# A sparse attention with two MLPs: the first block's weight conversion held to three units ahead of use, and the opening loads reordered

## The chip, the core and the metric

One NeuronCore of a Trainium2 chip. Five engines run their own instruction streams and meet at semaphores: PE (TensorE, matrix multiply), DVE (VectorE, elementwise), ACT (ScalarE, elementwise with functions), POOL (GpSimd) and SP (SyncE, which issues most DMAs). PEld is PE's weight load, which overlaps its matmuls. The metric is device time of one execution in microseconds (us), lower is better.

## The reference

```
scores = q @ k.T / sqrt(64)           # 4 batches, 8 heads, 576 positions, head size 64
heads 0-3: keep 0 <= i - j < 32       # local
heads 4-7: keep j <= i, i % 32 == j % 32   # strided
x  = softmax(scores) @ v              # as 2304 tokens x 512
x  = (s * relu(x @ w_in)**2 + b) @ w_out          # w_in 512x2048, w_out 2048x512, float64
out = ((x @ w_a) * (x @ w_b)) @ w_o2              # w_a, w_b 512x1536, w_o2 1536x512, float64
```

The weights arrive as float64 and are converted on the core, and every float32 product is made of three passes of a split high + low operand (`PASSES`).

## The kernel before

The 2304 tokens are cut into six blocks of 384. Block 0 holds positions 0 to 95 of the four batches, block 1 positions 96 to 191, and blocks 2 to 5 the rest of one batch each.

**First attention.** `first` computes block 0's attention, one batch at a time: `first_load` (L331) brings q and k (tile `fqk`) and v (`fv`) of a batch, 192 KB each; PE transposes them (`fps`), multiplies scores (`fss`), DVE and ACT make the softmax (`fpt`, L210 to L223), PE transposes that (`fpp`) and multiplies with v (`fpo`); the result is split into the high and low half of `x`.

**The first MLP** goes through the hidden dimension in 16 units of 128 columns (NF1 = 16). For block n and unit f, `h_mm` makes 12 matmuls into `h`, ACT takes relu and square, and the result is split into `gt` (ACT writes the high half, DVE the low one, L132); `o_mm` of unit f - 2 (AHEAD1 = 2) adds 12 matmuls into `acc`. PE's order is written out: h(f), then steps of the next block's attention, then acc(f - 2), then more attention steps, and each step follows the last PE instruction (`in_order`). The attention of block n + 1 is made of two generators, `local_gens` and `strided_gens`; for block 1 each has four pieces, spread over the 16 units. Their tiles are `qn`, `kn`, `vn`, `lpt` (local) and `sk`, `sv`, `spo`, `spTo` (strided), `pqk`, `pst`, `pss`, `ppt` and `po` in PSUM.

**The weights** of a unit are two raw tiles of 512 KB, one of w_in and one of w_out (`stage`, L139 and L144), each with two 32-bit words per value. `to_float32` turns a raw tile into a float32 tile: ACT scales the high word (L153), DVE shifts and merges (L157, L160, L163), and `split` writes the high half on ACT (L131) and the low half on DVE (L132) of a tile `w`. `next_weights` does this for the two tiles of the next unit and stages raw tiles up to two units further.

In the kernel before, `stage_next` runs twice first, with the four raw loads of units 0 and 1 on ACT's DMA queue; the q, k and v loads follow on SP's. After the first attention two units are converted, and in block 0 `next_weights` stands inside the order of unit f, with only one condition: it comes after the last batch of the first attention. The scheduler then orders each engine's instructions by readiness, except for what is tied by `tc.issue_after` or raised by `tc.high_priority`.

From block 1 on, streams convert the second MLP's weights and write them to DRAM (`convert_w2`), and sum columns (`column_sums`). The last part of the program is the second MLP (`ab_mm`, `o2_mm`), which is matmuls nearly alone.

Of the kernel before, what the change touches and what calls it, by code (L numbers as in the profile page):

```python
# [26 lines left out]
def sparse_attention_two_mlps(  # L27
# [22 lines left out]
    nc = tc.nc  # L50
    B, H, S, D = q.shape
# [16 lines left out]
    NF1 = FF1 // P  # L68
# [41 lines left out]
    last_pe, behind = [], []  # L110
# [20 lines left out]
        nc.scalar.activation(out=hi, in_=src, func=AF.Copy)  # L131
        return eng_lo.tensor_tensor(out=lo, in0=src, in1=hi.bitcast(F32), op=ALU.subtract)  # L132

    def stage(w, f, cols, pool, queue=nc.sync):

        r = pool.tile([P, DM, 2], U32, tag="w" if pool in (wpa, wpb) else "raw", name="raw")
        words = w.bitcast(U32)
        if cols:
            load = queue.dma_start(  # L139
                out=r.rearrange("p (k c) t -> p k (c t)", k=KD),  # L140
                in_=words[:, f * 2 * P:(f + 1) * 2 * P].rearrange("(k p) c -> p k c", p=P),
            )
        else:
            load = queue.dma_start(  # L144
                out=r.rearrange("p c t -> p (c t)"), in_=words[f * P:(f + 1) * P, :]
            )
        return r, load.ins
# [182 lines left out]
    def first_load(dst, src, bb):  # L330
        nc.sync.dma_start(out=dst, in_=src[bb, :, 0:QT, :].rearrange("h t d -> t h d"))  # L331
# [214 lines left out]
    wi, wo = {}, {}  # L546
# [164 lines left out]
        gens = [strided(n - 2, pair) for pair in range(2)]  # L711
        return overlapped(gens, 4), 2 + 13 * len(gens)

    AHEAD1, AHEAD2 = 2, 1
    NX = 3 * NF2 - 2 * NF1
    words = []
    last_load = None

    def stage_next():

        nonlocal last_load
        f = len(words)
        both = []

        for w, cols, pool in (
            (w_in, True, raw if f >= NF1 - 1 else wpa), (w_out, False, raw if f >= NF1 - 2 else wpb)
        ):
            with tc.issue_after(last_load) if last_load is not None else ExitStack():

                r, load = stage(w, f, cols, pool, nc.scalar if f < 2 else nc.sync)  # L730
            last_load = load if f >= 2 else None
            both.append(r)
        words.append(both)

    def next_weights():
        f = len(wi)
        while len(words) <= min(NF1 - 1, f + 2):
            stage_next()
        wi[f] = by_rows(to_float32(words[f][0], wpa, "w"))
        wo[f] = to_float32(words[f][1], wpb, "w")  # L740
# [22 lines left out]
    qks, vs = [], []  # L763
    for bb in range(B):
# [1 line left out]
            vf = slot(wpb, [QT, 2, H, D], "fv")  # L766
        vs.append(vf[:, bb % 2])
        qks.append(slot(wpb, [QT, 2, H, D], "fqk"))
    for _ in range(2):
        stage_next()  # L770
    for bb in range(B + 2):
        if bb < B:
            first_load(qks[bb][:, 0], q, bb)
            first_load(qks[bb][:, 1], k, bb)
        if bb >= 2:
            first_load(vs[bb - 2], v, bb - 2)
    banks = ((ps_acc, "acc"), (ps_a, "a"), (ps_acc, "acc"), (ps_a, "a"))
    gens = [first(bb, qks[bb], vs[bb], fmask, *banks[bb]) for bb in range(B)]
    live, step = list(range(B)), 0
    while live:  # L780

        live = [bb for bb in live if bb > step or next(gens[bb], gens) is not gens]
        step += 1
    for _ in range(2):
        next_weights()
    later = [
        Stream(convert_w2(), 3 * NF2 + 1, (NB - 2) * NF1 - 2), Stream(column_sums(), NF1 + 1, 2 * NF1 - 1)
# [2 lines left out]
    for n in range(NB):  # L790
# [12 lines left out]
        for f in range(NF1):  # L803
            order = ExitStack()
            if n == 0:

                order.enter_context(tc.issue_after(first_done[B - 1].ins))
                if len(wi) < NF1:
                    next_weights()
            gt = in_order(h_mm, n, f)  # L810
            for st in streams:
                st()
            queue.append((acc, gt, f, n))
            if len(queue) > AHEAD1:
                in_order(o_mm, *queue.pop(0))
            for st in streams:
                st()
            order.close()
            if n == NB - 1:
                while len(w2) < NX + 2 * (f + 1 - AHEAD1):  # L820
                    load_w2(len(w2))
            elif n:
                for st in later[:n]:
                    st()
# [50 lines left out]
```

## Time and profile before

| | |
|---|---|
| median of 3 runs | 1057.99 us (1057.22 to 1059.37) |
| the profiled execution | 1055.04 us |
| its span in the profile | 1053.3 us |
| PE busy | 993.7 us (94%) |
| DVE busy | 473.4 us (45%) |
| ACT busy | 462.5 us (44%) |
| POOL busy | 74.8 us (7%) |
| first matmul of block 0's first unit | 45.20 us |
| first matmul of block 1's first unit | 169.50 us |

Times in the trace are us from the start of the span. A line of a timeline gives start, duration, engine, line of the code, operation, tile written <- tiles read, shapes and count, and in brackets how long the engine had been idle before it and what ended that. The span is 1.7 us shorter than the execution it was taken from.

### The profile page before, as it was taken

How to read it: one execution, taken by the hardware profiler on the slowest of the kernel's cores; microseconds unless marked ns; L12 is line 12 of the kernel's file. 1: busy time of each engine (PE TensorE's matmuls, PEld its weight loads, DVE VectorE, ACT ScalarE, POOL GpSimd, SP SyncE). 2: the span in 40 equal slices, each digit the busy share in tenths (PEclk: the TensorE clock that was granted, in tenths of full speed). 3: DMA queues.
4: the chain of work that ended last, by engine and by line, in shares of the span. 5: the costliest groups of instructions: out<-in, count | busy, mean ns of one | idle time of the engine just before them, and what ended most of it. 6: DMA issues, size and time to landing. Idle time of an engine off the chain costs nothing.

```text
span 1053.3 us, 15817 instructions
## 1 busy us (share of the span) xinstructions
PE 993.7 (94%) x5984; PEld 932.9 (89%) x5984; DVE 473.4 (45%) x1246; ACT 462.5 (44%) x1291; POOL 74.8 (7%) x110
## 2 busy tenths in 40 slices
PE   4958699999999899999999999999999999999998
PEld 3747599999999889999999999999999999999997
DVE  5799642767778777766622221221211211211111
ACT  4787565665765667476532231311311311211212
POOL 4000000000223331200000000000000000000000
PEclk9988699999999999999999999999999999999999
DMA  9675212254654635554567720100200100000000
GB/s 189 201 240 185 76 39 71 81 170 129 196 152 146 183 125 147 153 174 148 174 207 234 254 85 1 50 11 1 60 1 1 61 1 1 30 1 1 30 1 30
DMA packets 109819, 106.37 MB, mean 101 GB/s; under 512 B 59568, under 2 KB 94640, under 8 KB 109744
## 3 DMA queue, kind: packets, MB, share of 16 engines
q1 hardware_dynamic: 103216, 84.39, 28.0%
q0 software_dynamic: 5184, 18.88, 4.6%
q10 hardware_dynamic: 1344, 2.10, 0.6%
q8 instruction: 47, 0.77, 0.3%
q14 instruction: 28, 0.23, 0.1%
HBM read 77.03 MB, written 28.31 MB: 100 GB/s over the span
## 4 chain that ended last, share of the span: by engine, by line
PE 80%; DVE 8%; ACT 5%; DMA 4%; issue 2%; POOL 0%; SPq 0%; ACTq 0%; DVEq 0%; POOLq 0%
PE acc L113 29%; PE h L113 16%; PE pb L113 14%; PE pa L113 14%; PE pss L113 2%; PE po L113 2%; DVE raw L163 2%; DVE w L132 2%; DVE raw L160 1%; PE ppt L116 1%; DMA xr<-o 1%; DVE raw L157 1%; DMA fqk<-in_q_dram 1%; PE fss L113 1%; ACT w L131 1%
## 5 line engine op out<-in xcount | busy, mean ns | idle before, releaser
L113 PE MATMUL h<-x,w 128*128 128x384 f32 x1152 | 225.7, 344 | 1.8 <-ACT r L560 1.2
L113 PE MATMUL acc<-gt,w 128*128 128x384 f32 x1152 | 223.5, 341 | 2.7 <-ACT o1s L586 2.7
L113 PEld LDWEIGHTS h<-x,w 128*128 128x128 f32 x1152 | 202.5, 191 | 5.9 <-ACT r L560 2.0
L113 PEld LDWEIGHTS acc<-gt,w 128*128 128x128 f32 x1152 | 199.9, 189 | 6.9 <-ACT o1s L586 3.4
L641 DVE TENSOR_TENSOR ab<-pb,ab 128x384 f32<-128x384 f32 x72 | 40.1, 557 | 306.6 <-ACT ab L640 306.6
L113 PE MATMUL pb<-x,w 128*128 128x384 f32 x864 | 164.8, 337 | 0.0
L113 PE MATMUL pa<-x,w 128*128 128x384 f32 x864 | 161.9, 334 | 0.8 <-ACT ab L640 0.8
L113 PE MATMUL acc<-w,abt 128*128 128x512 f32 x648 | 161.8, 393 | 0.0
L640 ACT ACTIVATE ab<-pa 128x384 f32<-128x384 f32 x72 | 35.4, 491 | 282.3 <-PE pa L113 282.2
L113 PEld LDWEIGHTS pb<-x,w 128*128 128x128 f32 x864 | 153.7, 188 | 6.1
L113 PEld LDWEIGHTS pa<-x,w 128*128 128x128 f32 x864 | 150.8, 188 | 1.6 <-ACT ab L640 1.4
L113 PEld LDWEIGHTS acc<-w,abt 128*128 128x128 f32 x648 | 120.5, 188 | 21.9
L560 ACT ACTIVATE r<-h 128x384 f32<-128x384 f32 x96 | 46.6, 486 | 115.5 <-PE h L113 115.2
L567 DVE TENSOR_TENSOR r<-r 128x384 f32<-128x384 f32 x80 | 48.6, 608 | 88.6 <-ACT gt L566 88.0
L132 DVE TENSOR_TENSOR abt<-ab,abt 128x384 fp32r<-128x384 f32 x72 | 40.2, 558 | 46.9 <-ACT abt L131 46.9
L131 ACT ACTIVATE w<-raw 128x512 fp32r<-128x512 f32 x68 | 44.9, 668 | 27.3 <-DVE raw L163 20.6
L132 DVE TENSOR_TENSOR w<-raw,w 128x512 fp32r<-128x512 f32 x68 | 46.4, 686 | 22.1 <-ACT w L131 21.6
L568 DVE TENSOR_TENSOR gt<-r,gt 128x384 fp32r<-128x384 f32 x80 | 54.1, 676 | 4.5
L131 ACT ACTIVATE abt<-ab 128x384 fp32r<-128x384 f32 x72 | 37.7, 524 | 40.2 <-DVE ab L641 40.2
L604 POOL DMA_DIRECT2D w2d<-w x36 | 20.0, 556 | 443.6 <-DVE w L132 370.0
L153 ACT ACTIVATE raw<-raw 128x512 f32<-128x512 f32 x68 | 45.1, 674 | 9.8 <-DMA raw<-in_moe_w_in_dram 7.8
L163 DVE SCALAR_TENSOR_TENSOR raw<-raw 128x512 uint32<-128x512 uint32 x68 | 46.8, 691 | 0.7
(109 smaller groups left out, 884.7 us busy)
## 6 DMA issues: line engine op xcount, KB each, us to landing
w2d<-w POOLq DMA_DIRECT2D x36, 512.0 KB, 5.1
w<-w2d SPq DMA_DIRECT2D x36, 512.0 KB
raw<-in_moe_w_out_dram SPq DMA_DIRECT2D x26, 512.0 KB
raw<-in_moe_w_in_dram SPq DMA_DIRECT2D x14, 512.0 KB
raw<-in_moe_w_a_dram SPq DMA_DIRECT2D x12, 512.0 KB
raw<-in_moe_w_b_dram SPq DMA_DIRECT2D x12, 512.0 KB
xr<-o SPq DMA_DIRECT2D x6, 768.0 KB
o<-o1s SPq DMA_DIRECT2D x20, 192.0 KB
```

Of the source, the lines that this page charges most:

```text
L113: last_pe[:] = [nc.tensor.matmul(*args, **kwargs).ins]
L116: last_pe[:] = [nc.tensor.transpose(*args).ins]
L131: nc.scalar.activation(out=hi, in_=src, func=AF.Copy)
L132: return eng_lo.tensor_tensor(out=lo, in0=src, in1=hi.bitcast(F32), op=ALU.subtract)
L153: nc.scalar.activation(out=high.bitcast(F32), in_=high.bitcast(F32), func=AF.Copy, scale=HIGH_SCALE)
L163: nc.vector.scalar_tensor_tensor(out=high, in0=high, scalar=0x80000000, in1=low, op0=ALU.bitwise_and, op1=ALU.bitwise_or)
L560: relu = nc.scalar.activation(out=r, in_=ph, func=AF.Relu)
L567: nc.vector.tensor_tensor(out=r, in0=r, in1=r, op=ALU.mult)
L568: lo = nc.vector.tensor_tensor(out=gt[:, 1], in0=r, in1=gt[:, 0].bitcast(F32), op=ALU.subtract)
L604: stores.append(nc.gpsimd.dma_start(out=w2d[i - 1], in_=w.bitcast(F32)).ins)
L640: nc.scalar.activation(out=ab, in_=pa, func=AF.Copy)
L641: nc.vector.tensor_tensor(out=ab, in0=pb, in1=ab, op=ALU.mult)
```

## The change

Three edits. The raw loads of units 0 and 1 move from ACT's queue to SP's, each behind two batches' q, k and v instead of ahead of all of them. Three units instead of two are converted between the first attention and the loop (EARLY = 3). In block 0 `next_weights` runs from unit 1 on, ahead of the condition on the first attention, and behind the relu and the split of the unit before (`behind`).

```diff
-            load = queue.dma_start(
+            load = nc.sync.dma_start(
...
-    AHEAD1, AHEAD2 = 2, 1
+    AHEAD1, AHEAD2, EARLY = 2, 1, 3
...
             with tc.issue_after(last_load) if last_load is not None else ExitStack():
-
-                r, load = stage(w, f, cols, pool, nc.scalar if f < 2 else nc.sync)
-            last_load = load if f >= 2 else None
+                r, last_load = stage(w, f, cols, pool)
             both.append(r)
...
-    for _ in range(2):
-        stage_next()
-    for bb in range(B + 2):
-        if bb < B:
-            first_load(qks[bb][:, 0], q, bb)
-            first_load(qks[bb][:, 1], k, bb)
-        if bb >= 2:
-            first_load(vs[bb - 2], v, bb - 2)
+    for bb in range(B):
+        first_load(qks[bb][:, 0], q, bb)
+        first_load(qks[bb][:, 1], k, bb)
+        if bb % 2:
+            first_load(vs[bb - 1], v, bb - 1)
+            first_load(vs[bb], v, bb)
+            stage_next()
...
-    for _ in range(2):
+    for _ in range(EARLY):
         next_weights()
...
             if n == 0:
+                if len(wi) < NF1 and f:
+
+                    with after(behind):
+                        next_weights()
 
                 order.enter_context(tc.issue_after(first_done[B - 1].ins))
-                if len(wi) < NF1:
-                    next_weights()
             gt = in_order(h_mm, n, f)
```

How the instructions stand now on the engines concerned. The first place is the head of SP's queue, before the change (`sb` are two scalars, `qn` and `kn` belong to block 1's first local piece, `fqk` and `fv` to the first attention; ACT's queue holds the four raw loads):

```order
L99 DMA sb<-in_moe_s_dram 128x1
L100 DMA sb<-in_moe_b_dram 128x1
L247 DMA qn<-in_q_dram 48x2x128
L251 DMA kn<-in_k_dram 64x2x128
L331 DMA fqk<-in_q_dram 96x8x64
L331 DMA fqk<-in_k_dram 96x8x64
L331 DMA fqk<-in_q_dram 96x8x64
L331 DMA fqk<-in_k_dram 96x8x64
```

and with it:

```order
L99 DMA sb<-in_moe_s_dram 128x1
L100 DMA sb<-in_moe_b_dram 128x1
L331 DMA fqk<-in_q_dram 96x8x64
L331 DMA fqk<-in_k_dram 96x8x64
L331 DMA fqk<-in_q_dram 96x8x64
L331 DMA fqk<-in_k_dram 96x8x64
L331 DMA fv<-in_v_dram 96x8x64 x2
L139 DMA raw<-in_moe_w_in_dram 128x4x256
L144 DMA raw<-in_moe_w_out_dram 128x1024
L331 DMA fqk<-in_q_dram 96x8x64
L331 DMA fqk<-in_k_dram 96x8x64
```

The first batch's q is SP's third load instead of its fifth, the small loads for block 1 are gone from the head, and the third batch's q and k stand behind one unit's raw loads.

The second place is DVE right behind the first attention, before the change (`raw_513` and `raw_515` are unit 2, `raw_531` and `raw_533` unit 3, `raw_553` unit 4):

```order
L157 TENSOR_SCALAR raw_513<-raw_513 128x512
L157 TENSOR_SCALAR raw_515<-raw_515 128x512
L157 TENSOR_SCALAR raw_531<-raw_531 128x512
L160 SCALAR_TENSOR_TENSOR raw_513<-raw_513 128x512
L160 SCALAR_TENSOR_TENSOR raw_515<-raw_515 128x512
L157 TENSOR_SCALAR raw_533<-raw_533 128x512
L160 SCALAR_TENSOR_TENSOR raw_531<-raw_531 128x512
L163 SCALAR_TENSOR_TENSOR raw_513<-raw_513 128x512
L163 SCALAR_TENSOR_TENSOR raw_515<-raw_515 128x512
L157 TENSOR_SCALAR raw_553<-raw_553 128x512
```

and with it (`gt_586` and `gt_641` are the splits of units 0 and 1):

```order
L163 SCALAR_TENSOR_TENSOR raw_515<-raw_515 128x512
L132 TENSOR_TENSOR w_557<-raw_513,w_557 128x512
L132 TENSOR_TENSOR w_564<-raw_515,w_564 128x512
L132 TENSOR_TENSOR gt_586<-r_584,gt_586 128x384
L157 TENSOR_SCALAR raw_531<-raw_531 128x512
L157 TENSOR_SCALAR raw_533<-raw_533 128x512
L160 SCALAR_TENSOR_TENSOR raw_531<-raw_531 128x512
L391 COPY skT_659<-pst_665 128x288
L160 SCALAR_TENSOR_TENSOR raw_533<-raw_533 128x512
L163 SCALAR_TENSOR_TENSOR raw_531<-raw_531 128x512
L163 SCALAR_TENSOR_TENSOR raw_533<-raw_533 128x512
L132 TENSOR_TENSOR gt_641<-r_639,gt_641 128x384
```

Unit 3's conversion now begins behind unit 0's split, where before it and unit 4's stood ahead of it.

The third place is DVE in the middle of block 0 with the change, behind the copy `spTo` of the second strided piece and up to unit 8's split `gt_1247` (`raw_944` is unit 9, `raw_1030` and `raw_1032` unit 10):

```order
L163 SCALAR_TENSOR_TENSOR raw_944<-raw_944 128x512
L160 SCALAR_TENSOR_TENSOR raw_1030<-raw_1030 128x512
L160 SCALAR_TENSOR_TENSOR raw_1032<-raw_1032 128x512
L132 TENSOR_TENSOR w_1110<-raw_942,w_1110 128x512
L163 SCALAR_TENSOR_TENSOR raw_1030<-raw_1030 128x512
L132 TENSOR_TENSOR w_1117<-raw_944,w_1117 128x512
L132 TENSOR_TENSOR x_597<-po_1166,x_597 128x192
L163 SCALAR_TENSOR_TENSOR raw_1032<-raw_1032 128x512
L132 TENSOR_TENSOR w_1222<-raw_1030,w_1222 128x512
L132 TENSOR_TENSOR w_1229<-raw_1032,w_1229 128x512
L391 COPY skT_1203<-pst_1209 128x288
L132 TENSOR_TENSOR gt_1247<-r_1245,gt_1247 128x384
```

Before the change all conversions were past this point when unit 8's split came. PE's order differs in the first attention alone; from block 0's first unit on it is the same, row for row.

## Rows read from the trace of the kernel before

**Rows 1.** The page's part 1: PE busy, share, instructions.

```profile
PE 993.7 (94%) x5984; PEld 932.9 (89%) x5984; DVE 473.4 (45%) x1246; ACT 462.5 (44%) x1291; POOL 74.8 (7%) x110
```

**Rows 2.** Busy time by stretch: PE, PEld, DVE, ACT, POOL; clock, DMA share, GB/s.

```profile
52.00:78.00 26.00, 13.47 (x85) 12.08 (x84) 26.00 (x65) 22.16 (x57) 0.00 (x0) 0.86 0.73 243
78.00:104.00 26.00, 21.74 (x133) 20.31 (x134) 25.01 (x62) 17.59 (x45) 0.00 (x0) 0.87 0.54 167
104.00:126.50 22.50, 12.17 (x69) 10.38 (x68) 16.94 (x35) 12.06 (x29) 0.00 (x0) 0.62 0.30 94
126.50:169.50 43.00, 43.00 (x310) 41.33 (x308) 16.04 (x60) 26.03 (x82) 0.00 (x0) 1.00 0.17 40
```

**Rows 3.** Timeline of PE, 45 to 126: waits and slow groups in block 0.

```profile
75.53 0.87 PE L116 MATMUL ppt<-ident,lpt 96*128 96x96 f32 x4 [9.71 <-ACT w L131]
...
91.49 0.74 PE L116 MATMUL pst<-ident,sk 96*128 96x96 f32 x3 [3.26 <-ACT kT L267]
91.93 3.66 PE L113 MATMUL h<-x,w 128*128 128x384 f32 x12
...
117.23 1.51 PE L116 MATMUL ppt<-ident,spo 96*96 96x96 f32 x8 [2.03 <-DVE spo L223]
...
121.84 4.02 PE L113 MATMUL acc<-gt,w 128*128 128x384 f32 x12
```

**Rows 4.** Busy time by stretch, behind the longest wait (columns as rows 2).

```profile
75.00:81.00 6.00, 3.93 (x18) 3.70 (x19) 6.00 (x11) 3.63 (x7) 0.00 (x0) 0.50 0.12 44
```

**Rows 5.** Timeline of PE, 0 to 50: first transposes, third batch's scores, first unit.

```profile
14.27 2.77 PE L116 MATMUL fps<-ident,fqk 96*128 96x96 f32 x12 [14.27 <-DMA fqk<-in_q_dram]
...
26.05 2.35 PE L113 MATMUL fss<-fqkT 64*96 64x96 f32 x16
...
45.20 4.48 PE L113 MATMUL h<-x,w 128*128 128x384 f32 x12 [0.58 <-ACT x L131]
```

**Rows 6.** Timeline of SP's DMA queue: start and length of an issue.

```profile
1.75 0.43 SPq L247 DMA_DIRECT2D qn<-in_q_dram  x1
...
6.19 0.33 SPq L331 DMA_DIRECT2D fqk<-in_q_dram  x1
```

**Rows 7.** Busy time by stretch: q, k and v loads; weight loads (columns as rows 2).

```profile
16.00:18.00 2.00, 1.93 (x13) 1.65 (x14) 0.00 (x0) 0.98 (x2) 0.00 (x0) 1.00 1.29 202
36.00:38.00 2.00, 2.00 (x20) 1.48 (x18) 1.47 (x11) 2.00 (x13) 0.00 (x0) 1.00 1.02 359
```

**Rows 8.** Timeline of DVE, 50 to 57: conversions back to back, a split.

```profile
50.95 0.69 DVE L163 SCALAR_TENSOR_TENSOR raw<-raw 128x512 uint32<-128x512 uint32 x1
51.55 0.42 DVE L157 TENSOR_SCALAR raw<-raw 128x512 uint32<-128x512 uint32 x1
51.89 0.69 DVE L160 SCALAR_TENSOR_TENSOR raw<-raw 128x512 uint32<-128x512 uint32 x1
52.49 0.69 DVE L132 TENSOR_TENSOR w<-raw,w 128x512 fp32r<-128x512 f32 x1
53.09 0.69 DVE L163 SCALAR_TENSOR_TENSOR raw<-raw 128x512 uint32<-128x512 uint32 x1
...
56.44 0.55 DVE L132 TENSOR_TENSOR gt<-r,gt 128x384 fp32r<-128x384 f32 x1
```

**Rows 9.** Timeline of ACT: two scalings of a unit's words.

```profile
42.92 1.23 ACT L153 ACTIVATE raw<-raw 128x512 f32<-128x512 f32 x2
```

**Rows 10.** Timeline of PE, 126 to 170: unit 8, last scores, block 1's first unit.

```profile
126.52 2.35 PE L113 MATMUL h<-x,w 128*128 128x384 f32 x12
...
159.08 0.82 PE L116 MATMUL ppt<-ident,spo 96*96 96x96 f32 x8
...
169.50 2.24 PE L113 MATMUL h<-x,w 128*128 128x384 f32 x12
```

**Rows 11.** Timeline of DVE, 126 to 131: waits once no conversion is left.

```profile
126.78 0.46 DVE L391 COPY skT<-pst 128x288 f32<-128x288 f32 x1 [4.11 <-PE pst L116]
...
130.55 0.56 DVE L132 TENSOR_TENSOR gt<-r,gt 128x384 fp32r<-128x384 f32 x1 [3.31 <-ACT gt L131]
```

More of the change, by code (lines that the diff above doesn't have):

```diff
@@ L132, in split, with stage @@
         return eng_lo.tensor_tensor(out=lo, in0=src, in1=hi.bitcast(F32), op=ALU.subtract)
-    def stage(w, f, cols, pool, queue=nc.sync):
+    def stage(w, f, cols, pool):
         r = pool.tile([P, DM, 2], U32, tag="w" if pool in (wpa, wpb) else "raw", name="raw")
@@ L143, in stage @@
         else:
-            load = queue.dma_start(
+            load = nc.sync.dma_start(
                 out=r.rearrange("p c t -> p (c t)"), in_=words[f * P:(f + 1) * P, :]
```

## The prediction

> **What bounds the kernel now.** The page first [rows 1]: PE is busy for 993.7 us, 94% of the span, so a change can gain only where PE stands still or runs slowly. The stretch table then shows where that is [rows 2]: PE is busy 13.47 of 26.0 us at 52 to 78, 21.74 of 26.0 at 78 to 104 and 12.17 of 22.5 at 104 to 126.5, 27.1 us idle in all, while DVE is full there (26.00 and 25.01 of 26). That is block 0, in which DVE converts 14 of the 16 units of the first MLP's weights. From 126.5 to 169.5 the picture is turned round: PE 43.00 of 43.00, DVE 16.04. Before 126.5 DVE is the bound, after it PE, and neither helps the other. PE's timeline shows why [rows 3]: the transposes of the next block's scores wait 9.71 us, and other transposes 3.26 us, because what they need stands on DVE and ACT behind conversions that no matmul needs yet. The clock adds to it. After the long wait the granted clock is 0.50, the lower of its two levels, 1.2 GHz [rows 4]; groups of twelve matmuls that take 2.24 us take 3.66 and 4.02 behind such waits [rows 3, 10].
>
> I count to one landmark: the first matmul of block 1's first unit, at 169.50 [rows 10]. PE's own order behind it is the same in both kernels, and DVE has room there, so what moves the landmark moves the end.
>
> **The start.** Before, the first transposes wait until 14.27 for q [rows 5]; its load was issued at 6.19, behind two small loads of a later step and in company with 2 MB of weights [rows 6]. In the changed order it is SP's third load; the third was issued at 1.75 [rows 6]. A 192 KB load takes 0.97 us at the 202 GB/s of such loads [rows 7], so with 2 us for its start and its signal, an estimate, q can be read near 4.7; the bound on the other side is the old 8.1 us from issue to use, so 9.8. What sets the pace next is k of the third batch: in front of it stand six loads (5.8 us), one unit of weights (1.05 MB at 359 GB/s [rows 7], 2.9 us) and its own pair (1.9 us), from about 3, so it can be used near 14.3. Twenty transposes follow before that batch's scores, at 2.77 / 12 us each [rows 5], 4.6 us: 18.9. By PE alone it is 4.7 + (26.05 - 14.27) + eight transposes pulled ahead (1.8) = 18.3. I take 18.6 where before has 26.05. From there to the last product took 44.62 - 26.05 = 18.6 us, now less four transposes (0.9): 36.3, and the first unit's matmuls start 0.6 later, at 36.9, instead of 45.20: **8.3 us** earlier. Between nothing and 9.6 is possible. Twelve DVE instructions of units 0 and 1 that lay ahead of the scores now lie among them, 6.2 us by rows 8; I cost them at nothing because PE is the busy engine in this stretch, and at 3 us if that cover fails. Unit 2 is new ahead of the loop, 4.3 us of DVE; it is done while PE works on unit 0, whose matmuls took 4.48 us at the start [rows 5] and will again: twice the 2.24 of rows 10, so at the lower level of the clock.
>
> **Block 0 by DVE.** A tile's conversion is one L157 and one each of L160, L163 and L132, in steps of 0.34, 0.60, 0.60 and 0.60 us [rows 8]: 2.14, a unit of two tiles 4.28. A unit's own split takes 0.55 [rows 8]. The scores of block 1 are four pairs of steps (one local, one strided); 126.5 to 169.5 holds two pairs and eight splits in 16.04 us [rows 2], so a pair is (16.04 - 4.4) / 2 = 5.8.
> Unit 0's split: 36.9 + 4.48 = 41.4, then the chain through ACT. Unit 8's matmuls end at 128.87 [rows 10] and its split starts at 130.55 [rows 11], 1.7 us; two conversions on ACT now stand inside it, 1.2 [rows 9]. It starts at 44.3 and ends at 44.8.
> Until unit 15 is converted DVE then has 13 units (55.6), 13 splits (7.2) and four pairs less the last one's copy and two splits of x (23.3 - 1.2 = 22.1): 84.9 us, up to 129.7 if it never waits.
> It will wait. Once a unit's conversions follow the split of the unit before, DVE can't run ahead of PE any more. The longest gap shows in before, as soon as DVE had no conversions left: 4.11 and 3.31 us idle from the copy of transposed scores to the next split [rows 11], because PE must do the products, an output group, transposes and the next unit's matmuls first. In the changed order nine instructions of 0.60 us stand in that gap (third piece of the order above), so 7.4 - 5.4 = 2.0 us remain, four times: 8.0. The bounds are 0 and 4 x 7.4. DVE ends unit 15 at 137.7; the last normalised scores stand two instructions, 1.4 us, ahead: 136.3.
>
> **The rest by PE.** From those transposes to block 1's first matmul took 169.50 - 159.08 = 10.4 us [rows 10]: 146.7. PE waits for those scores some 5 us, an estimate: behind unit 12's split DVE has about 7 us of work up to them, PE one output group of 2.2. That lies between the 3.26 and the 9.71 that were followed by slow groups [rows 3], so one burst at the lower level, 2.0 us (1.4 to 1.8 for one group of twelve by rows 3 and 10, and some small ones): 148.7.
> Sum: 169.5 - 148.7 = **20.8 us** less. Against the profiled execution, 1055.04, that is 1034.2; the median of the runs lies 2.95 above it, so 1037.2.
>
> Moved at no cost: the four weight loads, from the head of ACT's queue onto SP's, where they pace the second half of the q and k loads as counted. The later weight loads stay SP's, behind loads that wait for PE to release the small q, k and v tiles; they run some two units ahead of use, and a load takes 1.5 us at 359 GB/s, so I cost them at nothing. If one came late, ACT's next unit would wait behind it.
>
> **Rivals.**
> *PE becomes the bound at once.* Units 8 to 15 take PE 43.0 us without a gap [rows 10]; units 0 to 7 hold two output groups less, 38.8. 36.9 + 81.8 + the slow first group's 2.2 = 120.9; DVE's own floor is 129.7 - 1.4 + 10.4 = 138.7. So at best 31 us less, 1027 as a median, 1025 with an earlier start. For it: DVE's long order of ready work. Against: the chain through ACT in each unit.
> *Waits are traded for waits.* Each pair costs the whole 7.4 instead of 2.0, 21.6 us more, and the whole gain is gone, the start's with it: 1059; half of that leaves 10 less. For it: in before DVE never waited in this stretch, so no row shows the coupled order. Against: ACT is busy 22.16 of 26 us at worst [rows 2], and three units of lead cover one unit's chain three times over.
> *Slower: the clock.* Short waits in every unit leave PE at 1.2 GHz through block 0. Its 81.8 us become 81.8 x 1.9 = 155 (4.02 and 4.48 against 2.24 for a group; 1.51 against 0.82 for eight transposes, rows 3 and 10), and the landmark comes at 192, 22 us later: 1081. It decides against the change once two thirds of the block run so, since 36.9 + 132.6 reaches 169.5. For it: a wait of 3.26 us was enough for a slow group [rows 3]. Against: all but the last of the waits I count are near 2.0 us, as is the one of 2.03 in rows 3, and groups of full speed stand between them.
> The Trainium skill speaks for this one: "TensorE: Matmul & The Clock Gate", section "HAM oscillation — how this bites in real kernels", describes bursts of matmuls with waits between them that find the clock throttled again at every burst. By that page the sum would be 1081, by the rows 1037. The trace agrees that idle time lowers the clock (0.50 in rows 4), and shows it for single long waits, not for a whole block.
> *The change does less than it says.* If conversions were reordered on paper and DVE still filled first, nothing would change; the order of DVE rows speaks against it.
>
> **How the numbers follow.** Forecast (10 to 29 less) 0.70; PE or DVE without waits (29 to 36 less) 0.08; half the gain lost to waits (2 to 10 less) 0.12; within 0.2% (2.1 us, about what a measurement of this kernel can tell from none) 0.03; slower, clock or worse waits, 0.07. So faster 0.90, same 0.03, slower 0.07. For 8 in 10 I go from 1024, DVE hardly waiting and a start 2 us better, to 1048, half of the gain lost.
>
> **What would show it.** First transposes near 5, first unit's matmuls near 37, block 1's first matmul near 149. DVE no longer full at 52 to 78, nor PE idle for 7 us or more in block 0; lower clock in one or two stretches. I am wrong if block 0 keeps its 124 us from its first matmul, or if its output groups mostly take 4 us.

## The result and the profile after

The changed kernel takes 1040.56 us, the median of four runs (1038.47 to 1042.37); the kernel before took 1058.68 beside it (1057.22 to 1059.57, four runs). The ratio is 0.9829, with a 95% interval of 0.9807 to 0.9852: 18.1 us less. The profiled execution of the changed kernel took 1042.37 us with a span of 1040.5; that of before took 1055.04 with a span of 1053.3. So the two traces differ by 12.7 us only: the one of before lies 3.6 us below the median of its runs here, the one of after 1.8 above. Stages are compared by the traces, sizes by the medians.

The page's part 1 of the kernel after, busy time and share of the span:

```profile
PE 997.3 (96%) x5984; PEld 936.0 (90%) x5984; DVE 470.0 (45%) x1246; ACT 461.7 (44%) x1291; POOL 72.6 (7%) x110
```

The same instructions and nearly the same busy time as in [rows 1], in a shorter span. The busy time by stretch of the kernel after (PE, PEld, DVE, ACT, POOL; clock, DMA share, GB/s) shows where:

```profile
52.00:78.00 26.00, 18.75 (x121) 16.86 (x120) 22.10 (x58) 19.35 (x51) 0.00 (x0) 0.87 0.59 185
78.00:104.00 26.00, 22.51 (x148) 20.94 (x147) 24.29 (x62) 20.76 (x57) 0.00 (x0) 0.87 0.62 182
104.00:126.50 22.50, 22.50 (x163) 21.54 (x162) 18.50 (x51) 19.25 (x55) 0.00 (x0) 1.00 0.56 174
```

Against [rows 2] PE's idle time from 52 to 126.5 fell from 27.1 to 10.7 us, and DVE is no longer full from 52 to 78 (22.10 where it had 26.00). The timeline of PE of the kernel after, the start:

```profile
6.10 1.86 PE L116 MATMUL fps<-ident,fqk 96*128 96x96 f32 x8 [6.10 <-POOL smask L193]
...
20.35 2.35 PE L113 MATMUL fss<-fqkT 64*96 64x96 f32 x16
...
39.45 0.69 PE L113 MATMUL h<-x,w 128*128 128x384 f32 x1 [0.58 <-ACT x L131]
...
45.28 4.21 PE L113 MATMUL h<-x,w 128*128 128x384 f32 x12 [0.58 <-ACT r L560]
```

The first transposes come at 6.10 instead of 14.27, the third batch's scores at 20.35 instead of 26.05, the first unit at 39.45 instead of 45.20 [rows 5]. The row at 6.10 names POOL as the last releaser. That is a mask which nothing on PE reads; PE's instruction waits for the identity matrix and for q, and since the identity was there at 1.54 (the run with early matmuls below shows it), it must have waited for q. The timeline of PE of the kernel after, block 0's waits and the slow groups behind them:

```profile
59.70 2.02 PE L113 MATMUL h<-x,w 128*128 128x384 f32 x10 [1.27 <-DVE w L132]
...
66.02 0.52 PE L116 MATMUL ppt<-ident,lpt 96*128 96x96 f32 x4 [2.22 <-DVE lpt L223]
69.23 1.49 PE L116 MATMUL ppt<-ident,spo 96*96 96x96 f32 x8 [2.69 <-DVE spo L223]
70.42 3.90 PE L113 MATMUL h<-x,w 128*128 128x384 f32 x12
...
97.36 1.54 PE L113 MATMUL po<-spTo,sv 96*64 96x96 f32 x12 [1.45 <-DVE spTo L529]
98.83 3.41 PE L113 MATMUL acc<-gt,w 128*128 128x384 f32 x12
...
140.88 0.87 PE L116 MATMUL ppt<-ident,lpt 96*128 96x96 f32 x4 [5.41 <-DVE lpt L223]
141.75 1.49 PE L116 MATMUL ppt<-ident,spo 96*96 96x96 f32 x8
142.94 3.53 PE L113 MATMUL h<-x,w 128*128 128x384 f32 x12
...
153.94 2.24 PE L113 MATMUL h<-x,w 128*128 128x384 f32 x12
```

The wait of 9.71 us [rows 3] has become one of 2.22 and one of 2.69. Three times a group of twelve takes 3.4 to 3.9 us instead of 2.24 (and unit 1's group, at 45.28, takes 4.21 where it took 2.36 in before), and once PE waits for converted weights (1.27, at 59.70), which it never did before. Block 1's first matmul stands at 153.94 instead of 169.50 [rows 10], 15.56 us earlier. Of that 5.75 were won at the start; block 0, from its first matmul to block 1's, fell from 124.3 to 114.5 us. Its row, first of the kernel before (columns as above):

```profile
45.20:169.50 124.30, 96.22 (x609) 89.14 (x609) 90.79 (x233) 82.48 (x218) 0.00 (x0) 0.88 0.38 119
```

and of the kernel after:

```profile
39.45:153.94 114.49, 97.08 (x608) 90.31 (x609) 88.23 (x230) 82.14 (x218) 0.00 (x0) 0.91 0.47 143
```

PE's idle time in block 0 fell from 28.1 to 17.4 us, by 10.7. The same matmuls took 0.9 us more. So all of block 0's gain is less waiting, and the slow groups take a little of it back.

Behind this landmark the trace of after needs 886.6 us, that of before 883.8. About 1.5 of these 2.8 us can be seen, at the start of block 2. PE's timeline there, of the kernel after:

```profile
346.20 0.79 PE L113 MATMUL acc<-gt,w 128*128 128x384 f32 x3 [2.59 <-ACT o1s L586]
346.92 1.56 PE L113 MATMUL pss<-skT,sqT 64*84 64x126 f32 x12
348.41 3.22 PE L113 MATMUL h<-x,w 128*128 128x384 f32 x12
```

and of the kernel before, the same three groups:

```profile
361.41 0.79 PE L113 MATMUL acc<-gt,w 128*128 128x384 f32 x3 [2.30 <-ACT o1s L586]
362.13 0.94 PE L113 MATMUL pss<-skT,sqT 64*84 64x126 f32 x12
363.00 2.35 PE L113 MATMUL h<-x,w 128*128 128x384 f32 x12
```

The wait is there in both; behind it the matmuls of before run at full speed, and those of after are slow for a while. The length of the wait does not tell the two cases apart. With four units ahead (an experiment below) a shorter one is followed by a slower group:

```profile
342.12 0.79 PE L113 MATMUL acc<-gt,w 128*128 128x384 f32 x3 [2.20 <-ACT o1s L586]
...
343.78 3.81 PE L113 MATMUL h<-x,w 128*128 128x384 f32 x12
```

Of the fourteen traces of this case, twelve have the slow group there, behind waits of 2.17 to 2.71 us; only before (2.30) and six ahead (2.09) have not. So the 1.5 us are no price of the change: the trace of before is one of the two that were spared them. The other 1.3 us were not located, and from run to run the totals of either kernel differ by more.

### The profile page after: what moved, and what is told of

It reads as the page before. It is cut to its first block, busy times and chain, and to the rows that moved or that the text cites. A ratio compares the mean times of both kernels' runs of the same rounds, so it can differ in the third digit from the quotient of the medians.

```text
span 1040.5 us, 15811 instructions
## 1 busy us (share of the span) xinstructions
PE 997.3 (96%) x5984; PEld 936.0 (90%) x5984; DVE 470.0 (45%) x1246; ACT 461.7 (44%) x1291; POOL 72.6 (7%) x110
## 4 chain that ended last, share of the span: by engine, by line
PE 85%; DVE 6%; ACT 5%; DMA 3%; issue 1%; SPq 0%; ACTq 0%; DVEq 0%
PE acc L113 30%; PE h L113 18%; PE pb L113 14%; PE pa L113 14%; PE pss L113 2%; PE po L113 2%; PE ppt L116 2%; DMA o<-o1s 1%; DMA xr<-o 1%; PE fss L113 1%; DVE raw L160 1%; DVE w L132 1%; DVE raw L163 1%; DVE raw L157 1%; ACT r L560 1%
## 5 line engine op out<-in xcount | busy, mean ns | idle before, releaser
L113 PE MATMUL h<-x,w 128*128 128x384 f32 x1152 | 229.2, 348 | 3.4 <-DVE w L132 1.3
L113 PEld LDWEIGHTS h<-x,w 128*128 128x128 f32 x1152 | 205.4, 194 | 7.9 <-DVE w L132 1.6
L132 DVE TENSOR_TENSOR w<-raw,w 128x512 fp32r<-128x512 f32 x68 | 45.9, 685 | 21.7 <-ACT w L131 20.8
L163 DVE SCALAR_TENSOR_TENSOR raw<-raw 128x512 uint32<-128x512 uint32 x68 | 46.5, 686 | 0.7
L160 DVE SCALAR_TENSOR_TENSOR raw<-raw 128x512 uint32<-128x512 uint32 x68 | 45.9, 685 | 0.5
```

The costliest lines, as they stand in the source:

```text
L113: last_pe[:] = [nc.tensor.matmul(*args, **kwargs).ins]
L160: nc.vector.scalar_tensor_tensor(out=low, in0=high, scalar=3, in1=low, op0=ALU.logical_shift_left, op1=ALU.bitwise_or)
L163: nc.vector.scalar_tensor_tensor(out=high, in0=high, scalar=0x80000000, in1=low, op0=ALU.bitwise_and, op1=ALU.bitwise_or)
```

## The experiments

Each was timed beside the kernel before on the same chip; the medians of before beside them lie between 1058.6 and 1059.1 us, so the medians of the table can be compared with each other. The table gives, of each profile, unit 0's first matmul and block 1's first, PE's idle and busy time between these two, and then the median of the runs. PE has the same matmuls to do between the two in every kernel (20 more where waits are filled), so a longer busy time there means slower matmuls.

| kernel | unit 0 | block 1 | PE idle | PE busy | median, us | ratio to before (95%) |
|---|---|---|---|---|---|---|
| before | 45.20 | 169.50 | 28.1 | 96.2 | 1058.7 | |
| after (three ahead) | 39.45 | 153.94 | 17.4 | 97.1 | 1040.6 | 0.9807 to 0.9852 |
| hold alone | 44.88 | 161.52 | 17.8 | 98.8 | 1047.4 | 0.9869 to 0.9914 |
| loads alone | 39.59 | 164.37 | 27.1 | 97.6 | 1051.7 | 0.9926 to 0.9956 |
| two ahead | 39.41 | 162.55 | 20.4 | 102.7 | 1050.5 | 0.9909 to 0.9940 |
| four ahead | 39.49 | 149.52 | 13.3 | 96.7 | 1035.8 | 0.9772 to 0.9803 |
| five ahead | 39.37 | 148.43 | 13.2 | 95.9 | 1033.6 | 0.9746 to 0.9784 |
| six ahead | 39.45 | 152.15 | 18.3 | 94.4 | 1039.4 | 0.9798 to 0.9833 |
| three ahead, less DVE work | 39.47 | 147.66 | 12.8 | 95.4 | 1034.9 | 0.9762 to 0.9803 |
| four ahead, early matmuls | 38.96 | 147.84 | 14.1 | 94.8 | 1034.3 | 0.9749 to 0.9787 |
| five ahead, early matmuls | 38.83 | 147.91 | 13.6 | 95.5 | 1032.5 | 0.9733 to 0.9776 |
| five ahead, early matmuls, held behind the scores | 38.75 | 145.84 | 11.7 | 95.4 | 1030.8 | 0.9717 to 0.9761 |
| five ahead, early matmuls, waits filled | 39.14 | 146.77 | 10.7 | 96.9 | 1035.0 | 0.9757 to 0.9810 |
| six ahead, early matmuls, held behind the scores | 38.88 | 142.25 | 8.8 | 94.6 | 1029.0 | 0.9704 to 0.9738 |

Where an expectation speaks of the gelu, the relu and square of a unit is meant.

### The two parts apart

*The hold alone* keeps the loads of the kernel before and takes the rest of the change:

```diff
-    AHEAD1, AHEAD2 = 2, 1
+    AHEAD1, AHEAD2, EARLY = 2, 1, 3
...
+                if len(wi) < NF1 and f:
+
+                    with after(behind):
+                        next_weights()
...
-                if len(wi) < NF1:
-                    next_weights()
```

> The second part of the change alone: conversions of block 0 held to three units ahead, loads in the order and on the queues of the kernel before. Theory (two separate gains: the loads bring the first matmul of unit 0 about 5.75 us forward, the hold shortens block 0 by about 9.8 us, 124.3 to 114.5 between that matmul and block 1's first in the two profiles): unit 0's first matmul near 45, block 1's first near 160, total near 1049, between 1046 and 1052. Rival A (only the earlier start counts, the hold merely moves the waits): 1057 to 1059. Rival B (block 0 ends when VectorE has done its work, and the hold is the whole gain): 1040 to 1043.

Measured: 1047.4 us, 11.5 less than before by the ratio of 0.9891, and block 0 lasts 116.6 us, with 17.8 us of PE's idle time in it instead of 28.1. This is the theory, not either rival.

*The loads alone* take the loads of the change and leave the conversions as before (two ahead, no hold):

```diff
-    AHEAD1, AHEAD2, EARLY = 2, 1, 3
+    AHEAD1, AHEAD2, EARLY = 2, 1, 2
...
-                if len(wi) < NF1 and f:
-
-                    with after(behind):
-                        next_weights()
...
+                if len(wi) < NF1:
+                    next_weights()
```

> The first part of the change alone: q and k of the first positions lead on the sync queue and the weight words follow; conversions of block 0 are issued as early as in the kernel before, two of them ahead of the block. Theory (two separate gains): unit 0's first matmul near 39.5, total near 1053, between 1051 and 1055. Rival A (only the earlier start counts): 1040 to 1043. Rival B (the hold is the whole gain, the time won at the start is spent waiting in block 0): 1057 to 1059.

Measured: 1051.7, 6.2 us less than before by the ratio of 0.9941, unit 0 at 39.59, and block 0 lasts 124.8 us as it did before. Its row for 52 to 78 (columns as above) and the first rows of what PE waited for from 37 to 160 (total, times, longest) show the old picture:

```profile
52.00:78.00 26.00, 12.01 (x69) 10.90 (x69) 26.00 (x65) 20.54 (x50) 0.00 (x0) 0.76 0.74 257
```

```profile
PE ppt L116 <- DVE lpt L223: 15.1, 2, 7.6
PE ppt L116 <- DVE spo L223: 6.9, 2, 5.5
```

DVE is full, and PE waits 22 us for scores that stand behind conversions. The two gains add up: 11.5 and 6.2 make 17.7 of the 18.1 us. By the landmark it is 8.0 and 5.1 of 15.6 us, so 2.5 us come only with both or are scatter between the traces; these runs do not tell which. By either count somewhat over 60% of what the two give apart is the hold.

### How many units ahead

Only the number changes, EARLY = 2, 4, 5 and 6 instead of 3.

> The changed kernel with two conversions ahead of block 0 instead of three, so each unit's conversion is released one unit nearer to its use. If VectorE's work ahead of unit 0 holds the start: unit 0's first matmul comes up to 0.7 us earlier (x's low split stood behind the third conversion there), and 1039 to 1041. If the lead is what covers the wait for converted weights: each of the units 2 to 15 waits some more for its weights, 1042 to 1048. No effect at all: 1039.5 to 1042.

> The changed kernel with four conversions ahead of block 0. About 4.3 us of VectorE work more stands ahead of unit 0's first product or beside it. If the lead is what covers the waits of VectorE for the gelu (11.8 us of them in block 0): 1036 to 1040. If conversions ahead of the gelu's product and of the score work delay these: 1042 to 1046. No effect: 1039.5 to 1042.

> The changed kernel with five conversions ahead of block 0. With two, three and four the medians were 1050.5, 1040.6 and 1035.8. If lead goes on covering waits of PE: what is left of them in block 0 with four is 10.3 us in the score work (ppt, po) and none for weights, so a fifth finds little to cover: 1033 to 1036. If each further unit puts 4.3 us of VectorE work ahead of the first units' gelu splits and scores (with no hold at all the loads alone gave 1051.7): 1037 to 1041.

> Six conversions ahead. Lead covers on: 1031 to 1036. Conversions in front of the score work cost more than they cover, as in the kernel without a hold: 1038 to 1046, above the run with five.

Measured: 1050.5, 1035.8, 1033.6 and 1039.4. With two ahead the time is above the range that I gave for the theory that lead covers, 10 us slower than with three; with four it is 0.2 us below the range of the same theory, with five inside it; with six the other theory holds. What PE waited for from 42 to 160, with two ahead:

```profile
PE h L113 <- ACT w L131: 11.3, 4, 3.7
```

and with six ahead:

```profile
PE ppt L116 <- ACT w L131: 9.9, 1, 9.9
```

Two opposed waits shape the curve. With few units ahead PE waits for weights: 11.3 us with two, the 1.27 of the row at 59.70 with three, none from four on. With many ahead it waits for the first scores, which stand behind conversions on DVE and on ACT: the wait ahead of the first `ppt` is 2.22, 2.94, 5.33 and 9.87 us with three, four, five and six, and it was 9.71 in before [rows 3]. Three ahead pays for both. A third wait shrinks with lead: ahead of the last `ppt`, 5.41 us with three, 0.82 with four, none with five. The waits are not all: with two ahead PE is idle only 3.0 us longer in block 0 than with three (20.4 against 17.4) and busy 5.7 us longer (102.7 against 97.1), so most of what is lost there is lost to slow matmuls behind the waits. These numbers explain why four and five are better than three. Four and five are not told apart: PE is idle for 13.3 and 13.2 us, and their runs overlap (1034.9 to 1036.8 and 1031.7 to 1036.3). The first unit comes at the same time in all four; from three ahead on PE then waits some 0.7 us in it for x's low half, which it does not with two, and a fourth, fifth or sixth conversion costs nothing more there.

### Is DVE's work the bound?

One step of the conversion runs on 8 of its 512 columns, in the units converted inside block 0, which leaves out most of that step's work and leaves other numbers in the weights:

```diff
+        c = 8 if EARLY <= len(wi) - (pool is wpb) < NF1 else DM
...
         nc.vector.scalar_tensor_tensor(
-            out=high, in0=high, scalar=0x80000000, in1=low, op0=ALU.bitwise_and, op1=ALU.bitwise_or
+            out=high[:, 0:c], in0=high[:, 0:c], scalar=0x80000000, in1=low[:, 0:c],
+            op0=ALU.bitwise_and, op1=ALU.bitwise_or
         )
```

> The changed kernel; in the units converted inside block 0 (3 to 15, 26 instructions) the last step that joins sign and exponent with the mantissa runs on 8 of 512 columns, so those weights are other numbers; every wait stays. It takes 26 x 0.57 = 15 us of VectorE work from block 0. Theory (block 0 ends when VectorE's work and its waits have run, and TensorE has 16 us of idle time there): most of it is gained, block 1's first matmul at 140 to 146 instead of 153.94, total 1026 to 1033. Rival (TensorE or the low clock sets block 0): 1036 to 1040. Rival (VectorE waits for the gelu all the longer): no change, 1039 to 1042.

Measured: 1034.9, 5.7 us below the changed kernel, and block 1 at 147.66, 6.3 earlier. This lies between the theory's 1026 to 1033 and the rival's 1036 to 1040, and the landmark is a little beyond the theory's 140 to 146. The rows from 47.9 to 141, of the kernel after:

```profile
47.90:141.00 93.10, 76.95 (x506) 71.71 (x506) 80.67 (x216) 73.85 (x201) 0.00 (x0) 0.91 0.49 148
```

and with less work:

```profile
47.90:141.00 93.10, 81.56 (x543) 75.67 (x543) 69.80 (x220) 74.80 (x206) 0.00 (x0) 0.91 0.51 158
```

DVE's idle time rises from 12.4 to 23.3 us. The 26 shortened steps are busy for 3.9 us instead of 17.4, so 13.5 us were taken from DVE, and 6.3 come off at the landmark. Of these 6.3 only 4.6 are less waiting of PE (12.8 us in block 0 against 17.4); 1.7 are faster matmuls (95.4 against 97.1), and unit 1's group, which took 2.39 us here and 4.21 in after, lies ahead of the first shortened step. The rest turns into waits of DVE, most of them for ACT (13.1 us for the high half of a unit's split and 4.9 for that of weights, from 47.9 to 141). So DVE's work sets part of block 0, and less than half of what is taken from it is gained.

### TensorE's clock before the block

On the kernel with four ahead, six matmuls whose result nothing reads run on PE while q is on its way:

```diff
+    dummy = ps_h.tile([P, 2 * TU], F32, tag="h", name="dummy")
+    for _ in range(6):
+        nc.tensor.matmul(
+            dummy, lhsT=ident, rhs=qz.rearrange("p h t -> p (h t)"), start=True, stop=True
+        )
```

> The kernel with four conversions ahead and six matmuls of 128x384 (float32, result unused) on PE before q arrives. In the first attention PE is busy throughout from 20 to 37 us, at durations of the lower clock level (0.22 us for a 96x96 transpose, 0.12 later). If work on PE before it raises the clock and the first attention keeps it: the transposes there take 0.12, unit 0 starts 1 to 3 us earlier and its two first products take 2.3 us each instead of 5.3 and 4.2: 1029 to 1033. If the first attention's small matmuls don't keep the clock, or don't bring it: 1036 to 1038 (the six cost up to 1 us).

Measured: 1034.3, 1.5 us below four ahead without them (1035.8); the ranges of the two, 1031.8 to 1036.3 and 1034.9 to 1036.8, overlap, and it lies between the two cases of the expectation, so the total is inconclusive. The order of PE's steps in the first attention shifts a little with the added work, so that two batches' scores come ahead of the third batch's transposes. The timeline of PE of this run is clearer:

```profile
8.32 1.49 PE L116 MATMUL fps<-ident,fqk 96*128 96x96 f32 x16
9.78 2.18 PE L113 MATMUL fss<-fqkT 64*96 64x96 f32 x32
15.58 0.90 PE L116 MATMUL fps<-ident,fqk 96*128 96x96 f32 x4 [3.62 <-DMA fqk<-in_q_dram]
...
44.80 2.36 PE L113 MATMUL h<-x,w 128*128 128x384 f32 x12 [0.58 <-ACT r L566]
```

The first sixteen transposes take 0.09 us each; in the kernel after they took 0.23. Then PE waits 3.62 us for the third batch's q, and the next four take 0.22 each again. Its row for a stretch of the first attention:

```profile
20.00:26.00 6.00, 6.00 (x46) 4.98 (x45) 4.73 (x28) 6.00 (x28) 0.00 (x0) 0.50 0.88 229
```

PE has no idle time here and the granted clock is 0.50, 1.2 GHz, up to the first products of block 0. So the early matmuls did raise the clock, and it was back at the lower level behind one wait: 3.7 us of work ran at full speed, and then PE stood waiting for q, so that little of it reached unit 0. The second product takes 2.36 us where it took 4.21 in after, but it does so in before (2.36) and in the run with less DVE work (2.39) too, which have no early matmuls. The next experiment adds the same six to five ahead:

> Five conversions ahead and the six early matmuls together. If their gains are separate (five against four: 2.2 us; early matmuls: 1.5 us, 1035.8 to 1034.3): 1031 to 1033. If the first units' products no longer wait for TensorE's clock but for VectorE, which has a unit more to convert there: 1033 to 1035.

Measured: 1032.5 (1031.3 to 1035.4) against 1033.6 (1031.7 to 1036.3) without them: in the expected range, and not to be told from no change. Here the second product takes 4.21 again, so that the gain on that group is not steady either.

### Holding the conversions behind the scores

On five ahead with the early matmuls, no conversion at unit 1, and each later one behind the last two normalisations (`normal` collects the instruction of line 223):

```diff
-                if len(wi) < NF1 and f:
+                if len(wi) < NF1 and f > 1:
...
-                    with after(behind):
+                    with after(behind + normal[-2:]):
```

> As the run with five ahead and the early matmuls, with the hold set behind the scores: no conversion is released at unit 1, and from unit 2 on each stands behind the last two normalisations of block 1's scores as well. Theory (with five ahead, TensorE's waits of 5.3 and 3.6 us for the first normalised scores are steps of the conversion that stand ahead of the normalisation on VectorE and of the exponentials on ScalarE): these waits fall under 2 us each, and the total is 1023 to 1029. Rival (VectorE waits for the scores instead, and the conversions come later): 1031 to 1036.

Measured: 1030.8, 1.7 below the run without it, between the theory's 1023 to 1029 and the rival's 1031 to 1036; the runs of the two touch (1030.2 to 1032.3 and 1031.3 to 1035.4), so the size of the gain is uncertain. The mechanism did what was expected, at the first group of scores; PE's timeline of this run:

```profile
62.66 0.52 PE L116 MATMUL ppt<-ident,lpt 96*128 96x96 f32 x4 [0.54 <-DVE sm L230]
63.74 0.84 PE L116 MATMUL ppt<-ident,spo 96*96 96x96 f32 x8 [0.56 <-ACT w L131]
...
87.06 0.90 PE L116 MATMUL ppt<-ident,lpt 96*128 96x96 f32 x4 [2.94 <-DVE lpt L231]
90.49 0.91 PE L113 MATMUL po<-pT,vn 128*64 128x96 f32 x8 [2.52 <-ACT pT L301]
...
95.99 4.21 PE L113 MATMUL acc<-gt,w 128*128 128x384 f32 x12
```

The waits of 5.3 and 3.6 us are 0.54 and 0.56, and PE stays at full speed there. Then, with what had been held back, four units' conversions instead of three stand on DVE between the two groups' normalisations, and PE waits 2.94 and 2.52 us and falls to the lower clock. Of the 7.2 us by which the product behind the first group is ahead of the run without this hold (64.36 against 71.54), 2.1 are left at block 1.

The last run takes six ahead and begins the held conversions at unit 3:

> As the run with the hold behind the scores, with six conversions ahead and the first of the loop at unit 3. There the first group of scores no longer waited, the second waited 2.9, 2.5 and 0.8 us, and VectorE stood idle for 3.1 us ahead of the first scores. If the sixth conversion fits into that idle time and the conversions behind the scores are thereby less crowded: 1027 to 1030. If it delays the first scores, as six without that hold did (a wait of 9.9 us), or the second group waits as before: 1030 to 1034.

Measured: 1029.0 (1028.5 to 1030.1), as expected, and the fastest kernel here: some 11.5 us below the changed kernel and 2.8% below the kernel before. Its timeline of PE:

```profile
61.94 0.52 PE L116 MATMUL ppt<-ident,lpt 96*128 96x96 f32 x4 [1.26 <-DVE lpt L231]
62.81 0.84 PE L116 MATMUL ppt<-ident,spo 96*96 96x96 f32 x8 [0.34 <-ACT r L571]
...
87.11 0.91 PE L113 MATMUL po<-pT,vn 128*64 128x96 f32 x8 [2.25 <-ACT pT L301]
...
142.25 2.24 PE L113 MATMUL h<-x,w 128*128 128x384 f32 x12
```

Six ahead without that hold had the wait of 9.87 us in the same place, and 18.3 us of idle time in block 0 where this run has 8.8. So lead and cover for the scores can be had together, if the lead is made before the scores are ready and not beside them. The busy time from 45 to 142 says it in one line each, first of the kernel before:

```profile
45.00:142.00 97.00, 68.72 (x402) 62.74 (x402) 81.79 (x200) 67.40 (x173) 0.00 (x0) 0.84 0.44 141
```

of the kernel after:

```profile
45.00:142.00 97.00, 80.57 (x518) 75.07 (x519) 82.25 (x218) 76.32 (x207) 0.00 (x0) 0.91 0.48 146
```

and of the last run:

```profile
45.00:142.00 97.00, 89.50 (x595) 83.20 (x596) 81.69 (x217) 77.39 (x211) 0.00 (x0) 0.93 0.51 153
```

DVE is busy for 82 us in each, and PE gets 402, 518 or 595 matmuls done in the same time. Not all of that is the order of DVE's work, since the last two kernels start unit 0 some 6 us earlier. But the hold alone, on the loads of before, gets 523 done in this stretch, with DVE busy for 78.5 us.

### Filling two waits

On five ahead with the early matmuls, matmuls without a reader ahead of the first two groups of transposes (`qz_` is `qz` read as 384 columns):

```diff
+        if n == 1 and hp_ == c0 == 0:
+            for _ in range(6):
+                mm(ppt.rearrange("p a q -> p (a q)"), lhsT=ident, rhs=qz_, start=True, stop=True)
...
+            if h == pair == i == 0:
+                for _ in range(4):
+                    mm(ppt.rearrange("p a b q -> p (a b q)"), lhsT=ident[:, :QT], rhs=qz_, start=True, stop=True)
```

> As the run with five ahead and the early matmuls, with matmuls whose result is not used in the two longest waits of TensorE in block 0: six of 128x384 (float32) ahead of the first transposes of local scores, four ahead of the first of the other scores. They should fit into waits of 5.3 and 3.6 us. If idle TensorE is what brings the lower clock there: the transposes behind them take 0.49 and 0.82 us instead of 0.87 and 1.49, the first product of the next unit 2.3 instead of 3.2, total 1 to 3 us below the run without them. If the clock falls all the same, or the fillers delay the transposes: no change or up to 2 us slower.

Measured: 1035.0 (1033.0 to 1039.3), 2.5 us above the run without them, where 1 to 3 below were expected. The mechanism is there, in PE's timeline of this run:

```profile
65.26 0.52 PE L116 MATMUL ppt<-ident,lpt 96*128 96x96 f32 x4 [1.50 <-ACT w L131]
...
69.74 0.84 PE L116 MATMUL ppt<-ident,spo 96*96 96x96 f32 x8 [1.38 <-DVE spo L231]
70.36 2.33 PE L113 MATMUL h<-x,w 128*128 128x384 f32 x12
```

The transposes take 0.52 and 0.84 us instead of 0.87 and 1.49, and the product behind them 2.33 instead of 3.21, and the granted clock from 52 to 78 is 1.00 instead of 0.80, so it was the idle time that lowered the clock there. Yet little is left of it. At the next output group the run is 1.9 us ahead (73.93 against 75.87), of which it had 0.6 at the first transposes already (65.26 against 65.87), and at block 1's start it is 1.1 ahead (146.77 against 147.91). At block 2's start it is 0.1 (339.66 against 339.75); the slow group behind the wait there is in both. Where the rest of the lead goes, and whether the fillers make the kernel slower at all, is not settled: the runs of the two overlap (1033.0 to 1039.3 and 1031.3 to 1035.4).

## Why the prediction was right, and where its sum was off

The forecast was 1037.2 us (1024 to 1048), 20.8 less by the landmark; measured were 1040.6, 18.1 less. The direction, the mechanism and the range held. By its steps:

- **The start: 8.3 us, measured 5.75**, the worst term. Three steps share the 2.55 us. The load of q took 4.36 us from its issue (1.74) to its use (6.10), not 3. I had given it the whole rate of such loads, but three more of its size were issued in the 3.3 us behind it, and the bytes moved by 6.10 are more than its own; that they share the rate is read from this, not tried by itself. From there to the third batch's scores it took 14.25 against 13.9. From those to the first unit 19.10 against 18.3: the last batch's scores came in two halves with transposes between them and took 3.05 us from start to start where before took 2.27. PE as the busy engine of this stretch was right. In the first of the three the 2 us for a load's start and signal were an estimate from no row; together with the loads behind it this load had 3.4.
- **Unit 0's chain: 7.4 us from its first matmul to its split, measured 7.9** (39.45 to 47.33); within it PE waited 0.68 us for x's low half, which stood behind a step of a conversion; with two ahead that wait is absent, so it was unit 2's. I had costed unit 2 at nothing, and its cover held but for that.
- **DVE's work and waits: 92.0 us from unit 0's split to the last scores' transposes, measured 94.4** (47.33 to 141.75). Here two errors met. The work was 82.0 us (94.4 less the waits) where I had 84.0 (unit 0's split and the 84.9, less the two steps behind the scores, which did stand there); about half of the difference is that a split takes DVE 0.47 us from its start to the next step's (133.96 to 134.43), not 0.55, and the rest was not located. The waits were 12.4 us, by the row for 47.9 to 141, where I had 8.0. They came where I had put them, and were longer and less even than four times 2.0: 3.2 us up to unit 1's split, then 3.1, 4.4 and 1.3 between the copy `spTo` of one piece and the split behind the copy `skT` of the next. The longest of each, in DVE's timeline:

```profile
54.66 0.56 DVE L132 TENSOR_TENSOR gt<-r,gt 128x384 fp32r<-128x384 f32 x1 [1.70 <-ACT gt L131]
...
76.65 0.62 DVE L132 TENSOR_TENSOR x<-po,x 128x192 fp32r<-128x192 f32 x2 [2.05 <-ACT x L131]
...
107.90 0.56 DVE L132 TENSOR_TENSOR gt<-r,gt 128x384 fp32r<-128x384 f32 x1 [4.27 <-ACT gt L131]
...
127.85 0.56 DVE L132 TENSOR_TENSOR gt<-r,gt 128x384 fp32r<-128x384 f32 x1 [1.28 <-ACT gt L131]
```


- **The tail by PE: 12.4 us with a slow burst, measured 12.2** (141.75 to 153.94). The wait that I had at some 5 us was 5.41, and the burst came.
- **Behind the landmark: nothing, measured 2.8 us in the traces**, of which 1.5 are the slow group at block 2's start, which the trace of before happens to lack.

The weight loads that moved cost nothing, as counted: from 36 to 160 no engine waits for one in after, where in before ACT waited 4.2 us for them.

In all the landmark came at 153.94 where I had 148.7, 5.2 us late: 2.6 from the start, 0.5 from unit 0, 2.4 from DVE's waits, less 0.2. The medians nevertheless differ by 18.1 us, more than the 15.6 by which the landmark moved: the profiled execution of before is 3.6 us faster than the median of its runs, and the gain of every kernel here is larger by the medians than by the landmark against that trace. So the time came 3.4 us from the forecast and the landmark 5.2, and that the time came nearer is luck.

Of the rivals, *PE bound at once* fell: PE still has 10.7 us of idle time from 52 to 126.5. *Waits traded for waits* fell as a whole: the hold alone gained 11.5 us. But it is the cost of the number chosen: PE's wait for weights, 1.27 us with three ahead, is 11.3 with two, and there the hold gains 1.2 us at most (1050.5 against 1051.7 for the loads alone, with ratios whose intervals overlap). *The clock* did not decide with three ahead, where block 0's matmuls took 0.9 us more than before; with two ahead it did most of the harm (5.7 us more than with three). And it was under-counted: three bursts at the lower clock behind waits and not one, by the rows at 70.42, 98.83 and 142.94, and unit 1's slow group besides. I had argued that waits near 2 us are too short to lower it. A pair of 2.22 and 2.69 with four transposes between them did it. The Trainium skill ("TensorE: Matmul & The Clock Gate", section "HAM oscillation — how this bites in real kernels") describes a kernel with a wait ahead of every burst of matmuls, whose bursts each find the clock throttled; here that is so at the three places where PE waits most, and not between them, where the clock is 1.00 (104 to 126.5).

That *the change does less than it says* fell with DVE's row for 52 to 78, 22.10 us of 26 instead of 26.00: conversions did move.

## What to carry to other kernels

When an engine that is not the bound of the whole kernel holds up the one that is, ask for the order of its work before its amount: here DVE was busy for 82 us of 97 in the slowest and in the fastest kernel. Prefetched work has a best distance, since it waits for its user when it is too late and stands in front of other users when it is too early; a sweep of that one number gave 7 us more than the first choice, and letting the short, awaited work go first moved the best distance outward, from five or fewer to six (seven was not tried), and gave 3.5 more (1032.5 to 1029.0). A load that is needed first is worth its place in the queue, but allow for the loads issued right behind it, which here seem to have shared its rate.

## What the runs showed of the hardware

- The record of the granted clock reads 1.00 for the first 50 us of the kernel after, though its matmuls there take the times of the lower clock: 0.23 us for a transpose that takes 0.09 in the run with early matmuls, 4.21 for a group of 2.24. In that run the record shows 0.50 for the same stretch, once the clock had risen and fallen. In these traces, before the first change of the clock, the durations tell it and the record does not.
- PE without any idle time, at 20 to 26 us, stayed at 0.50 as long as it did the transposes and the small products of the first attention; the early matmuls of 128x384, ahead of it, took 6.94 us, and the transposes right behind them ran at 0.09 us each.
- At block 2's start PE waits for ACT in every trace here, 2.09 to 2.71 us. In twelve of fourteen the next unit's group of twelve is slow (2.72 to 4.16 us), in two it runs at full speed (2.35 and 2.37). A wait of 2.17 us stands among the slow ones and one of 2.30 among the fast ones, so its length alone does not decide.
- The first load of 192 KB was usable 4.36 us after its issue, with three more of that size issued behind it; from 4 to 6 us the core's DMA moved 220 GB/s:

```profile
4.00:6.00 2.00, 0.00 (x0) 0.00 (x0) 0.00 (x0) 0.00 (x0) 2.00 (x9) 1.00 1.12 220
```

This row of the kernel after (columns as in the stretch rows above) is 0.44 MB, more than two such loads.
